# Selective attention followed by a hard-swish MLP: queries of four head pairs in another order, and three loads and one small step moved

## The chip, the cores and the metric

The kernel runs on one core of one Trainium2 chip. The metric is the device time of one execution in microseconds. A core has five engines that work side by side, each through its own instructions in order: PE (matrix multiplication, with PEld for the loading of its weights), DVE (vector operations), ACT (activation functions), POOL (general operations, and the issuing of some transfers) and SP (which issues transfers only). An engine that needs another's result waits for a semaphore. Matrix products land in PSUM, a small memory from which only DVE and ACT copy results to the main on-chip memory, SBUF.

## The reference

The inputs q, k and v have 8 batches, 8 heads, 576 tokens and 64 numbers a token; s has one number per batch, head and token. What is computed, cut to what matters:

```python
scores = q @ k^T / 8
cum = cumsum(max(s, 0))                        # per head, along the tokens
bias = -(cum[query] - cum[key])
scores = where(key > query, -1e9, scores + minimum(bias, 0))
attn = softmax(scores)
x = (attn @ v), heads side by side             # [4608, 512]
h = x @ w_in                                   # [4608, 2048]
out = (h * clip(h + 3, 0, 6) / 6) @ w_out      # [4608, 512]
```

## The kernel before, in words

**Tiling.** The 64 heads are worked on as 32 pairs, p = 0 to 31; a batch has four pairs (PPB = 4). All is in half precision. For a head the scores stand transposed, keys on the partitions and queries along the row: `scores(p, hh, g)` makes them in three parts, g = 0 for the four diagonal blocks of 128 keys by 128 queries, g = 1 and 2 for the blocks beside the diagonal; `corner(p)` makes the last 64 by 64 block of both heads. ACT takes the exponential of each part (L355, L393) into the tile P. `av(p, hh, part)` multiplies P with the values (and a column of ones, which gives the sums), `norm` divides (L434, L435, on DVE), and `transpose_x(p)` turns the result so that it can be the MLP's input xT (five PE transposes, L449, and a DVE copy, L454). In the MLP, `m1` makes one block of 128 features by 512 tokens (L478), ACT and DVE apply the gate (L493, L494), and `m2` multiplies with w_out (L505).

**The mask and the bias.** For p < 8 (NPROD) the causal mask is added by a matmul: `ident2`, twice the identity, times `shut`, a tile of 640 columns that holds -65504 where the key comes after the query (L318 for the four diagonal blocks, L374 for the corner). The bias comes from four extra rows of q and k, on partitions 64 to 67 of the tiles qk: for the queries the cumulative sum and ones, for the keys minus one and the sum in three parts. These rows lie ready for 32 heads in `rows_of` (slot 0 for queries, slot 1 for keys) and `load_aug(p)` fetches them with two transfers, one per head (L151). Pair 0 does without them: its bias comes from matmuls with `picked`, a copy of the query rows with all but one head's rows at zero. `pick(1)` makes the second head's (L712).

**From q and k to the tiles qk.** `load_qk` brings the tokens of a pair in with two transfers (L116). For p < 11 each of 96 partitions holds six tokens in a row per head. `transpose_in` turns them with six PE transposes per operand, two tokens at a time (L242), so that in PSUM the even tokens of each two lie on partitions 0 to 63 and the odd ones on 64 to 127. `transpose_out` then brings them in order with two copies, one for each half (L259): a copy reads a PSUM row in steps and writes every second element of the row of qk. For queries both copies are on DVE. For keys the first is on ACT and the second on DVE; both write to the same stretch of qk, and the second waits for the first. Pair 0 uses `head_out`, which does the same for one head (L273).

**The order of the work** is written out by hand in the loop over p. For p < 4 a pass holds attention alone: scores, `get(0)` (the query copies of pair p + 1), the corner, the last two steps of pair p - 1 (`av`, `norm`), `get(1)` (the key copies of p + 1), the second head's scores, and `transpose_x(p - 1)`. From p = 4 on the steps of the MLP are put between them by `group()`, after a list `plan`. PE, ACT and DVE work through what this order gives them.

**Transfers.** Two queues matter. POOL issues q and k, w_in and w_out and most of the bias rows, and between these it converts V to half precision (`cast_v`, L195 and L196). SP issues V (`load_v`, three transfers per pair, into two buffers in turn, so that V of p + 2 waits for the conversion of p), the bias rows of pairs 2 and 3, and later the outputs. What waits at the head of such a queue holds up all that stands behind it.

Of the kernel before, what the change touches and what calls it, by code (L numbers as in the profile page):

```python
# [18 lines left out]
def kernel(  # L19
# [10 lines left out]
    nc = tc.nc  # L30
# [61 lines left out]
    shut = keep("shut", [128, 640], F16)  # L92
# [3 lines left out]
    rows_of = keep("rows_of", [128, 2, 640], F16, 2)  # L96
# [12 lines left out]
    def load_qk(p, i):  # L109
        b, h0 = p // PPB, 2 * (p % PPB)  # L110
        src = (q, k)[i][b, h0 : h0 + 2]
        if not flat(p):
            if not i:
                tok = work.tile([128, 24 * D], F16, tag="tok", bufs=4, name="tok")
                toks[p] = tok[0:96].rearrange("p (i h e d) -> p i h e d", i=2, h=2, e=6)
            nc.gpsimd.dma_start(  # L116
                out=toks[p][:, i].rearrange("p h e d -> p h (e d)"),
                in_=src.rearrange("h (p e) d -> p h (e d)", e=6),
            )
        else:  # L120
            if p < NSW:
                if not i:
                    tok = work.tile([128, 24 * D], F16, tag="tok", bufs=4, name="tok")
                    toks[p] = tok[:, 0 : 18 * D]
                to, eng = toks[p], nc.gpsimd
            else:
                to, eng = raws[p % NRAW], nc.sync
            eng.dma_start(
                out=to.rearrange("p (i t d) -> p i t d", i=2, t=9)[:, i],
                in_=src.rearrange("h s d -> (h s) d").rearrange(  # L130
                    "(t p) d -> p t d", p=128
                ),
            )
# [14 lines left out]
    def load_aug(p, eng):  # L148
        for hh in range(2):
            g = 2 * p + hh  # L150
            eng.dma_start(  # L151
                out=qks[p % NQK][64:68, hh, :, 64 * hh : 64 * hh + SEQ],
                in_=rows_of[g // 32].rearrange("(r g) i t -> g r i t", g=32)[
                    g % 32, :, :, 0:SEQ
                ],
            )
# [72 lines left out]
    def transpose_in(p, i):  # L229
        tok = toks[p]  # L230
        pt = t_bank(i == 1 and p != NPROD, "pt")
        if flat(p):
            for c in range(5):
                c0 = 512 * i + 128 * c
                nc.tensor.transpose(
                    pt[:, 128 * c : 128 * (c + 1)], tok[:, c0 : c0 + 128], ident
                )
            return pt
        for hh in range(2):
# [8 lines left out]

    def transpose_out(
# [6 lines left out]
        copies = (nc.scalar.copy if i else copies[0], copies[1])  # L256
        for par in pars:
            to = qk[0:64, 0, i, par : par + SEQ]
# [11 lines left out]
    def head_out(p, i, hh, pt, copies):  # L270
        to = qks[p % NQK][0:64, hh, i, 64 * hh : 64 * hh + SEQ]
        for par in range(2):
# [28 lines left out]
    def by_rows(p, hh, out, keys, queries, stop=False):  # L301
        mm(
            out,
            lhsT=rows_of[0][:, 1, keys],
            rhs=picked[:, 2 * p + hh, queries],
            start=False,
            stop=stop,
        )

    def scores(p, hh, g):  # L310
# [4 lines left out]
        if g == 0:  # L315
            rows = slice(0, 68 if by_product else 128)
            if by_product:
                mm(S, lhsT=ident2, rhs=shut[:, 0:512], start=True, stop=False)  # L318
# [13 lines left out]
        else:  # L332
# [10 lines left out]
            if p < NROW:  # L343
                for j in ((0, 3) if g == 1 else (1, 2)):
# [4 lines left out]
                        lhsT=rows_of[0][:, 1, 128 * j : 128 * (j + 1)],  # L349
# [19 lines left out]
    def corner(p):  # L369
# [3 lines left out]
        if by_product:  # L373
            mm(  # L374
                S.rearrange("p h c -> p (h c)"),
                lhsT=ident2,
                rhs=shut[:, 512:640],
# [66 lines left out]
    def transpose_x(p):  # L444
# [3 lines left out]
        for t in range(5):  # L448
# [3 lines left out]
                ident,  # L452
# [155 lines left out]
    fill(nc.gpsimd, shut, 0.0)  # L608
    for c in (slice(0, 512), slice(512, 640)):
        w = 128 if c.start == 0 else 64  # L610
        part = shut[:, c].rearrange("p (t c) -> p t c", c=w)
# [3 lines left out]
            pattern=[[0, (c.stop - c.start) // w], [1, w]],  # L615
# [4 lines left out]
        )  # L620

# [24 lines left out]
    fill(nc.gpsimd, rows_of[0][:, 0, :], 1.0)  # L646
    fill(nc.gpsimd, rows_of[0][:, 1, SEQ:640], 0.0)
# [21 lines left out]
    fill(nc.vector, qks[0][64:68, 0, :, :], 0.0)  # L669

# [15 lines left out]
    def cum3(n, copy, cols):  # L686
        copy(out=rows_of[n][:, 1, cols], in_=C["c"][:, cols])

    def cum4(n, eng, cols):
# [3 lines left out]
            in1=rows_of[n][64:128, 1, cols],  # L693
# [3 lines left out]
    def cum5(n, copy, cols):  # L697
        copy(out=rows_of[n][64:128, 1, cols], in_=C["r"][64:128, cols])

    def cum6(n, eng, cols):  # L700
        lo = rows_of[n][96:128, 1, cols]
# [9 lines left out]
    def pick(g):  # L711
        nc.vector.tensor_scalar(  # L712
            out=picked[:, g, :],
            in0=rows_of[0][:, 0, 0:SEQ],
# [22 lines left out]
    fill(nc.gpsimd, rows_of[0][0:32, 1, 0:SEQ], -1.0)  # L737
# [9 lines left out]
    nc.gpsimd.tensor_copy(out=rows_of[0][0:32, 0, 0:SEQ], in_=C["c"][0:32])  # L747
# [4 lines left out]
    head_out(0, 1, 0, pts[1], (V.tensor_copy, V.tensor_copy))  # L752
    head_out(0, 0, 1, pts[0], (A, V.tensor_copy))
    head_out(0, 1, 1, pts[1], (V.tensor_copy, V.tensor_copy))
    warm(NWARM[2])
    for g in range(1, 2 * NROW):
        pick(g)
# [7 lines left out]
    load_aug(3, nc.sync)  # L765
    cast_v(1)
    for i in range(2):
        load_qk(4, i)

# [3 lines left out]
    for p in range(NP):  # L773
# [9 lines left out]
        if p == 1:  # L783
            load_aug(4, nc.gpsimd)
        elif p == 2:
# [4 lines left out]
        elif p == 3:  # L790
            cast_v(3)
            load_w_in(1)
            qk_ahead()
            load_aug(6, nc.gpsimd)
            cast_v(4)
        elif p:
# [42 lines left out]
        if p and p + 2 < NP:  # L839
            load_v(p + 2, nc.sync)  # L840
        if p == 2:
            nc.sync.dma_start(out=stair_sb, in_=stair_dram.ap())
        if p == 10:
            load_s(1, (nc.sync,) * 4)
            fill(nc.gpsimd, rows_of[1][:, 0, :], 1.0)
# [96 lines left out]
        elif p == 12:  # L942
            nc.scalar.copy(out=rows_of[1][0:32, 0, 0:SEQ], in_=C["c"][0:32])
            cum3(1, nc.scalar.copy, whole)
            fill(nc.gpsimd, rows_of[1][0:32, 1, 0:SEQ], -1.0)
# [44 lines left out]
```

The softmax here doesn't subtract the row's maximum and nothing guards it: scores larger than these inputs give would overflow.

## Time and profile before

| what | value |
|---|---|
| time, median of 3 runs | 356.13 us |
| lowest and highest of the 3 | 356.01 and 356.15 us |
| the profiled run | 356.22 us |
| its span in the trace | 354.5 us |
| clock that PE was granted | 1.00 of full speed |
| passes p = 0 to 3, attention alone | until about 27 us |
| last transfer of w_out that the MLP needs | landed at 61.9 us |

The span is what the trace covers; a run takes some 1.7 us more. A page of the profile gives the busy time of each engine, and then rows of groups of instructions: source line, engine, operation, tile written <- tiles read, the shapes (partitions x elements), the count, and after the bar the busy us in all, the mean ns of one, and the engine's idle us just before them with what ended it. In a timeline a row begins with the start and the length in us, and an idle time before it stands in brackets, with the instruction that ended it.

### The profile page before, as it was taken

To read this page: it belongs to the slowest core of one execution; us is meant where nothing else is said; L and a number is where in the kernel's file an instruction comes from. 1 tells how busy PE (TensorE), PEld (TensorE's weight loads), DVE (VectorE), ACT (ScalarE), POOL (GpSimd) and SP (SyncE) were. 2 spreads that over 40 slices of the span, in tenths; PEclk is the share of its full clock that TensorE was granted. 3 is DMA by queue.
4 is the path that set the end of the run, shared out by engine and by line. 5 is a ranking of instruction groups with operands and counts; after the bars stand their busy time and mean duration, and the time that the engine had idled before them with its cause. 6 is when DMAs were issued, how large, how long until landed. Compare 5 with 4: busy or idle time off the path is not lost.

```text
span 354.5 us, 7771 instructions
## 1 busy us (share of the span) xinstructions
PE 345.6 (97%) x2926; PEld 191.5 (54%) x2926; DVE 231.5 (65%) x472; ACT 225.4 (64%) x397; POOL 169.6 (48%) x295
## 2 busy tenths in 40 slices
PE   7889999999999999999999999999999999999995
PEld 3676666655555555555555555555555444444442
DVE  7898897677878677666666665757654553544531
ACT  6897896787787666667766666666664344433310
POOL 8987799666779556555555555555310000000000
PEclk9999999999999999999999999999999999999999
DMA  9999999999999999998788969997120100101111
GB/s 164 156 219 209 186 184 175 104 187 183 146 126 140 190 219 187 160 214 178 174 176 189 179 162 187 175 176 164 39 75 12 59 31 31 59 2 59 59 58 63
DMA packets 144438, 48.35 MB, mean 136 GB/s; under 512 B 130696, under 2 KB 139432, under 8 KB 144400
## 3 DMA queue, kind: packets, MB, share of 16 engines
q1 hardware_dynamic: 117088, 37.52, 53.4%
q0 software_dynamic: 27072, 10.05, 25.4%
q8 instruction: 23, 0.38, 0.5%
q10 hardware_dynamic: 240, 0.28, 0.2%
q14 instruction: 15, 0.12, 0.1%
HBM read 37.36 MB, written 9.44 MB: 132 GB/s over the span
## 4 chain that ended last, share of the span: by engine, by line
PE 90%; DVE 4%; ACT 3%; issue 1%; DMA 1%; ACTq 0%
PE po L505 34%; PE ph L478 34%; PE O L412 8%; PE S L336 7%; PE S L321 4%; DVE qk L259 1%; PE pt L242 1%; ACT P L355 1%; PE ptx L449 1%; DMA s_all<-in_s_dram 1%; DVE x L435 1%; PE S L318 1%; ACT tr L493 1%; DVE qk L219 1%; PE Sc L385 0%
## 5 line engine op out<-in xcount | busy, mean ns | idle before, releaser
L494 DVE SCALAR_TENSOR_TENSOR gT<-tr,ph 128x512 f16<-128x512 f32 x144 | 98.9, 687 | 97.4 <-ACT tr L493 96.3
L478 PE MATMUL ph<-xT,w_in_sb 128*128 128x512 f16 x576 | 148.1, 379 | 0.0
L505 PE MATMUL po<-w_out_sb,gT 128*128 128x512 f16 x576 | 145.8, 379 | 0.0
L493 ACT ACTIVATE tr<-ph,bias 128x512 f32<-128x512 f32 x144 | 99.1, 688 | 73.0 <-PE ph L478 70.6
L355 ACT ACTIVATE P<-S 128x512 f16<-128x512 f32 x192 | 111.4, 596 | 37.4 <-PE S L321 22.2
L478 PEld LDWEIGHTS <-w_in_sb 128*128 128x128 f16 x576 | 51.6, 97 | 44.2
L505 PEld LDWEIGHTS <-gT 128*128 128x128 f16 x576 | 50.2, 97 | 46.4 <-issue 0.2
L359 POOL TENSOR_SCALAR_AFFINE_SELECT P<-P 128x512 f16<-128x512 f16 x48 | 31.2, 650 | 45.2 <-ACT P L355 45.1
L336 PE MATMUL S<-qk 68*128 68x448 f16 (+3 forms) x256 | 49.0, 272 | 0.3 <-ACT P L355 0.2
L412 PE MATMUL O<-va,P 128*128 128x65 f16 x896 | 47.9, 193 | 0.3 <-ACT P L355 0.3
L412 PEld LDWEIGHTS <-P 128*128 128x128 f16 x896 | 39.3, 97 | 14.0 <-ACT P L355 0.5
L219 DVE COPY qk<-jt 64x768 f16<-64x768 f16 x84 | 36.6, 437 | 1.2
L336 PEld LDWEIGHTS <-qk 68*128 68x128 f16 x256 | 23.7, 98 | 24.2 <-issue 0.7
L151 POOL DMA_DIRECT2D qk<-rows_of x58 | 34.1, 591 | 2.8 <-PE S L336 1.6
L435 DVE TENSOR_TENSOR x<-O,rl 128x320 f16<-128x320 f32 x64 | 31.5, 492 | 2.2
L521 DVE TENSOR_SCALAR ob<-po 128x512 f32<-128x512 f32 (+1 forms) x36 | 24.4, 676 | 8.3 <-PE po L505 7.6
L259 DVE COPY qk<-pt 64x576 f16<-64x576 f16 x30 | 24.0, 805 | 6.4 <-ACT qk L259 5.3
L359 POOL TENSOR_SCALAR_AFFINE_SELECT PC<-PC 128x128 f16<-128x128 f16 x24 | 7.1, 294 | 41.0 <-ACT PC L393 40.9
L321 PEld LDWEIGHTS <-qk 128*128 128x128 f16 (+1 forms) x256 | 18.9, 98 | 12.7 <-DVE qk L259 0.8
L321 PE MATMUL S<-qk 128*128 128x128 f16 (+1 forms) x256 | 24.8, 219 | 0.0
L195 POOL CAST va<-vraw 128x512 f16<-128x512 f32 x32 | 21.2, 664 | 3.4 <-DMA vraw<-in_v_dram 3.3
L191 POOL CAST tok<-raw 128x576 f16<-128x576 f32 x28 | 18.1, 681 | 0.0
(71 smaller groups left out, 197.4 us busy)
## 6 DMA issues: line engine op xcount, KB each, us to landing
out_dram<-ob SPq DMA_DIRECT2D x35, 256.0 KB, 2.2
vraw<-in_v_dram SPq DMA_DIRECT2D x64, 128.0 KB, 3.8
raw<-in_q_dram SPq DMA_DIRECT2D x14, 288.0 KB, 3.7
raw<-in_k_dram SPq DMA_DIRECT2D x14, 288.0 KB
tok<-in_q_dram POOLq DMA_DIRECT2D x18, 144.0 KB, 4.9
tok<-in_k_dram POOLq DMA_DIRECT2D x18, 144.0 KB, 6.0
w_in_sb<-in_moe_w_in_dram POOLq DMA_DIRECT2D x4, 512.0 KB, 8.7
w_out_sb<-in_moe_w_out_dram POOLq DMA_DIRECT2D x8, 256.0 KB, 7.4
```

The source lines that it names most:

```text
L151: eng.dma_start(out=qks[p % NQK][64:68, hh, :, 64 * hh : 64 * hh + SEQ], in_=rows_of[g // 32].rearrange("(r g) i t -> g r i t", g=32)[g % ...
L219: copies[par](out=qk[0:64, :, i, 128 * par : 128 * par + 256 * n].rearrange("p h (s two c) -> p h s two c", two=2, c=128)[:, :, :, 0, :], ...
L321: mm(S[:, c], lhsT=kT[rows, c], rhs=qT[rows, c], start=(j == 0 and not by_product), stop=(j == 3 and p >= NROW),)
L336: mm(S[:, c : c + w], lhsT=kT[0:68, 128 * j : 128 * (j + 1)], rhs=qT[0:68, 128 * (j + 1) : SEQ], start=(c == 0), stop=(c != 0 and p >= NROW),)
L355: nc.scalar.activation(out=pt[:, c], in_=S, func=AF.Exp, scale=0.125)
L359: nc.gpsimd.affine_select(out=part, in_=part, pattern=[[0, part.shape[1]], [1, w]], compare_op=ALU.is_ge, fill=0.0, base=0, channel_multip ...
L412: mm(o[:, i, :], lhsT=lhsT, rhs=va[:, hh, j, 0:65], **kw)
L435: nc.vector.tensor_tensor(out=X[p][:, :, hh, :], in0=o[:, :, 0:64], in1=rl.to_broadcast([128, 5, 64]), op=ALU.mult,)
L478: mm(ph, lhsT=w_in_sb[:, kc, ft * 128 : (ft + 1) * 128], rhs=xT[:, kc, n * 512 : (n + 1) * 512], start=(kc == 0), stop=(kc == NKC - 1),)
L493: nc.scalar.activation(out=tr, in_=ph, func=AF.Relu, bias=bias3[:, 0:1])
L494: nc.vector.scalar_tensor_tensor(out=gTs[n][:, ft, :], in0=tr, scalar=6.0, in1=ph, op0=ALU.min, op1=ALU.mult)
L505: mm(po, lhsT=gTs[n][:, ft, t4 * 128 : (t4 + 1) * 128], rhs=w_out_sb[:, ft, :], start=(ft == 0), stop=(ft == NFT - 1),)
```

## The change

It has four parts.

1. **Queries of pairs p = 3 to 6 in another order.** `mixed(p, i)` is true for i = 0 (queries) and these pairs. `load_qk` now puts four tokens in a row on each partition, three times, both heads as one run of 1152 tokens. The six PE transposes write runs of 16 columns in steps of 32, and the two copies out of PSUM read one contiguous row and write runs of 16. Within each group of 64 queries, token 4v + w then stands at place 16w + v. The order of the keys stays. The mask in this order is a second tile, `shutm`; the query rows of the bias in this order are a third slot of `rows_of` (slot 0 is now the new order, 1 the old, 2 the keys), written by a POOL copy. In `transpose_x` the identity is replaced by a permutation matrix `perm`, which puts the queries back. The mask tiles shrink to 128 columns and are read four times (or twice, 64 columns) in one matmul.
2. **Keys of pairs p = 2, 4 and 6.** The first copy, which was one ACT copy of both heads, becomes an ACT copy of head 1 and a DVE copy of head 0.
3. **The second picking** moves ahead of the copies of pair 0's second head.
4. **Queues.** On SP the bias rows of pair 3 no longer stand ahead of V of pair 3, but behind it, and are followed by the rows of pair 4, which POOL issued before. On POOL the second part of w_in moves behind the tokens and rows of pair 6.

```diff
-    shut = keep("shut", [128, 640], F16)
+    shut, shutm = keep("shut", [128, 128], F16, 2)
+    perm = keep("perm", [128, 128], F16)
-    rows_of = keep("rows_of", [128, 2, 640], F16, 2)
+    rows_of = keep("rows_of", [128, 3, 640], F16, 2)
...
+            if mixed(p, i):
+                nc.gpsimd.dma_start(
+                    out=toks[p][:, i]
+                    .rearrange("p h e d -> p (h e d)")
+                    .rearrange("p (t x) -> p t x", t=3),
+                    in_=src.rearrange("h s d -> (h s) d").rearrange(
+                        "(t p e) d -> p t (e d)", p=96, e=4
+                    ),
+                )
+                return
...
-                    g % 32, :, :, 0:SEQ
+                    g % 32, :, slice(0, 3, 2) if mixed(p, 0) else slice(1, 3), 0:SEQ
...
+        if mixed(p, i):
+            for t in range(3):
+                for c in range(2):
+                    nc.tensor.transpose(
+                        pt[:, 0:SEQ].rearrange("p (g c v) -> p c g v", c=2, v=16)[
+                            :, c, 6 * t : 6 * t + 6
+                        ],
...
+    def mixed(p, i):
+        return i == 0 and PPB - 1 <= p < NPROD - 1
...
-        copies = (nc.scalar.copy if i else copies[0], copies[1])
+        if i and (p % 2 or p >= NPROD):
+            copies = (nc.scalar.copy, copies[1])
+        elif i:
+            head_out(p, i, 1, pt, (nc.scalar.copy,), (0,))
+            head_out(p, i, 0, pt, (nc.vector.tensor_copy,), (0,))
+            pars = (1,)
         for par in pars:
+            if mixed(p, i):
+                to = qk[0:64, 0, i, 16 * par : 16 * par + SEQ]
+                copies[par](
+                    out=bass.AP(
+                        to.tensor,
+                        to.offset,
+                        [list(to.ap[0]), [2 * SPAD + 64, 2], [32, 18], [1, 16]],
+                    ),
+                    in_=pt[64 * par : 64 * par + 64, 0:SEQ].rearrange(
+                        "p (h g v) -> p h g v", h=2, v=16
+                    ),
+                )
+                continue
...
-                mm(S, lhsT=ident2, rhs=shut[:, 0:512], start=True, stop=False)
+                mm(
+                    S.rearrange("p (t c) -> p t c", c=128),
+                    lhsT=ident2,
+                    rhs=(shutm if mixed(p, 0) else shut)[:, None, :].to_broadcast(
+                        [128, 4, 128]
+                    ),
...
-                ident,
+                perm if mixed(p, 0) else ident,
...
+    make_shut(shut, shut, [[1, 128]])
+    make_shut(shutm, mix(shutm), [[64, 2], [1, 4], [4, 16]])
+    nc.gpsimd.tensor_copy(out=unmix(perm), in_=mix(ident))
...
     fill(nc.vector, qks[0][64:68, 0, :, :], 0.0)
+    fill(nc.vector, rows_of[0][:, 0, :], 1.0)
...
     head_out(0, 1, 0, pts[1], (V.tensor_copy, V.tensor_copy))
+    for g in range(1, 2 * NROW):
+        pick(g, V)
     head_out(0, 0, 1, pts[0], (A, V.tensor_copy))
     head_out(0, 1, 1, pts[1], (V.tensor_copy, V.tensor_copy))
     warm(NWARM[2])
-    for g in range(1, 2 * NROW):
-        pick(g)
...
     load_v(2, nc.sync)
-    load_aug(3, nc.sync)
     cast_v(1)
     for i in range(2):
         load_qk(4, i)
+    nc.gpsimd.tensor_copy(
+        out=mix(rows_of[0][0:32, 0, 0:SEQ]), in_=unmix(C["c"][0:32])
+    )
...
-        if p == 1:
-            load_aug(4, nc.gpsimd)
-        elif p == 2:
+        if p == 2:
...
             cast_v(3)
-            load_w_in(1)
             qk_ahead()
             load_aug(6, nc.gpsimd)
+            load_w_in(1)
             cast_v(4)
...
             load_v(p + 2, nc.sync)
+        if p == 1:
+            load_aug(3, nc.sync)
+            load_aug(4, nc.sync)
```

## The prediction

> Pairs are counted by the index p of the code, from 0; the regrouped queries are those of p = 3 to 6. An arrow gives times before and after the change; the times after are all worked out here.
>
> **What bounds the kernel now.** First the page's busy shares, then busy time by stretch, cut where PE starts a pair's scores.
>
> ```profile
> PE 345.6 (97%) x2926; PEld 191.5 (54%) x2926; DVE 231.5 (65%) x472; ACT 225.4 (64%) x397; POOL 169.6 (48%) x295
> ...
> 14.26:18.42 4.16, 3.77 (x74) 3.04 (x71) 3.62 (x7) 4.01 (x9) 3.63 (x7) 1.00 1.25 217
> 18.42:22.68 4.26, 3.81 (x75) 3.02 (x71) 4.08 (x9) 3.84 (x9) 4.26 (x8) 1.00 1.24 214
> 22.68:26.94 4.26, 3.80 (x74) 3.01 (x70) 4.08 (x9) 3.84 (x9) 2.69 (x6) 1.00 1.25 219
> ...
> 120.00:340.00 220.00, 220.00 (x1654) 116.28 (x1653) 132.54 (x261) 130.23 (x221) 74.28 (x138) 1.00 0.60 122
> ```
>
> The columns are the stretch, its length, then busy us of PE, PEld, DVE, ACT and POOL. From 42 us on PE is the bound; in the attention-only stage it isn't, DVE is fullest. Busy PE hides waits, so I summed start-to-start times of consecutive matmuls less columns/2.4 + 2.5 ns: 338.4 us of work and 10.0 us of slack, of which 3.25 lie before 10 us, 1.57 in 10 to 20, 1.64 in 20 to 30, 1.04 in 30 to 40, and 2.5 in all the rest. A change that takes no matmul away can only get at these.
>
> Second, the timeline of DVE over one such pair, p = 2:
>
> ```profile
> 18.63 0.46 DVE L454 COPY xT<-ptx 128x576 f16<-128x576 f16 x1
> 19.01 0.18 DVE L434 RECIPROCAL rl<-O 128x5 f32<-128x5 f32 x1
> 19.23 0.49 DVE L435 TENSOR_TENSOR x<-O,rl 128x320 f16<-128x320 f32 x1
> 19.64 1.63 DVE L259 COPY qk<-pt 64x576 f16<-64x576 f16 x2
> 21.30 0.20 DVE L434 RECIPROCAL rl<-O 128x5 f32<-128x5 f32 x1
> 21.53 0.49 DVE L435 TENSOR_TENSOR x<-O,rl 128x320 f16<-128x320 f32 x1
> 22.05 0.81 DVE L259 COPY qk<-pt 64x576 f16<-64x576 f16 x1
> 22.89 0.46 DVE L454 COPY xT<-ptx 128x576 f16<-128x576 f16 x1
> ```
>
> No wait stands in it: the items fill 18.63 to 22.89, exactly the 4.26 us period. ACT waits 0.42 us a pair for the scores. Third, what PE waits for:
>
> ```profile
> 11.93 0.19 PE L302 MATMUL Sc<-w_out_sb,rows_of 128*128 128x64 f16 x1 [0.65 <-DVE w_out_sb L712]
> ...
> 22.07 0.28 PEld L449 LDWEIGHTS <-x 128*128 128x128 f16 x5 [0.72 <-DVE x L435]
> ...
> 26.33 0.28 PEld L449 LDWEIGHTS <-x 128*128 128x128 f16 x5 [0.73 <-DVE x L435]
> ```
>
> The first is p = 0's corner waiting for the second picking (L712). The others are the transposes of x, waiting for a normalisation that stands on DVE behind the two query copies. In matmul starts these gaps are 0.82, 0.61 and 0.62 us, with one of 0.55 at 17.19.
>
> Last, the rows with durations by shape:
>
> ```profile
> L259 DVE COPY qk<-pt 64x576 f16<-64x576 f16 x30 | 24.0, 805 | 6.4 <-ACT qk L259 5.3 <-PE pt L242 0.6
> L454 DVE COPY xT<-ptx 128x576 f16<-128x576 f16 x9 | 4.1, 454 | 0.6 <-PE ptx L449 0.5
> L273 DVE COPY qk<-pt 64x288 f16<-64x288 f16 x5 | 2.4, 480 | 0.6 <-ACT qk L273 0.5
> ```
>
> L259 and L454 copy 576 half-precision elements out of PSUM. The one whose rows run on takes 454 ns, the one that steps through both sides 805.
>
> **What the Trainium skill says.** "VectorE: DVE Perf Modes", section "Why PSUM operands drop a tier": a PSUM source allows at most the packed mode of two results a cycle. "Vector Engine (DVE) Microarchitecture Reference", section 5.1, gives the condition: every tensor of 2 bytes with innermost step one. L454 against L259 agrees, 351 ns apart; that runs of 16 are enough on the written side no row here shows. "TensorE: Matmul & The Clock Gate", section "Wait — 56ns, not 53.3ns?": warm matmuls start every N/2.4 + 2.5 ns; from 270 to 340 us the slack by that formula is under 0.05 us in all, so it holds. Its Part 4: a transpose is in.T @ identity; a permutation in the identity's place keeps the shape, so I take the 219 ns of L449 and no change in spacing. The six query transposes (L242) stay six of 96 columns; that they now write runs of 16 I cost at nothing, since PE waits for DVE right behind them.
>
> **The change, part by part.**
>
> *Queries, p = 3 to 6.* Two DVE copies a pair now read a contiguous PSUM row and write runs of 16. Their spacing is 0.815 us (1.63/2); in packed mode I take L454's 0.454 and 0.01 between: 0.70 us less per pair. Bounds: 0.93 less, were one copy 0.35 (at the 0.96 GHz of the skill's DVE page, two a cycle, the elements alone are 0.30); nothing less, if runs of 16 miss the mode. They run in the loop pass before their own pair: passes 2, 3, 4, 5.
>
> *Keys, p = 2, 4, 6.* The first half of the key copy, 0.80 us on ACT, becomes one head on ACT (0.47, L273) and one on DVE (0.48 to 0.50): ACT wins 0.33, DVE loses 0.50. The second half on DVE, which waits for both, may start 0.33 sooner where ACT was the last.
>
> *Second picking.* L712 (0.57 us) moves ahead of head 1's copies. DVE idles 0.46 us there (waiting for ACT's copy), ahead of the copies at 9.77, so it starts at 9.30, ends at 9.87 and pushes them by 0.07.
>
> *Masks, perm, rows.* PE's mask matmuls keep 512 and 128 columns: nothing. On POOL at the start 1.33 us of filling and selecting become about 1.15 (two fills of 0.15, two selects of 0.29, a copy like them). Were the three-level select twice as slow, the next loads would slip 0.1 us, against 0.9 of margin for tok of p = 1 (landed 9.29, read 10.24). The new fill of rows_of on DVE (0.33, as L177's 0.30 for 288 words) lands in the 0.35 us that DVE waits before the scan at 4.72: nothing, at most 0.05. The regrouped bias rows cost POOL one cast, 0.68 (L747) to perhaps 1.5; it takes the place of two 0.59 issues of p = 4's rows.
>
> *Sync and POOL queues.* V of p = 3 goes out when its buffer is freed, 14.27 → about 13.35. Behind it stand rows of 3, which now wait for POOL's cast (about 15.6), rows of 4, then V of 4 (17.37 → 18.0) and the stair. Rows of 3 then land near 20 (3.3 us, the median of these transfers) and are read at 22.5. V of 4 landed at 25.9, so now near 26.5; read at 30.4. The second w_in load moves behind tok and rows of 6, in a queue that lands its transfers in order: 29.89 → about 31.5, read at 35.7 less the gain. The regrouped query loads have 288 pieces for 192; tok of 5 and 6 arrive 4 to 5 us early. All of it is hidden.
>
> *The path.* p = 0: PE goes on when head 1's copies are done, 11.35, so the next transposes start 11.96 → 11.45: **-0.51**. p = 1: DVE starts the queries of 2 at 15.38 → 14.88, but its chain gets 0.50 of keys, and the copy that the scores of 2 await ends at 18.61 as before: **+0.51**, and ACT waits longer. p = 2: normalisation 22.02 → 21.27, so PE transposes when its own work is done, at 21.47. The keys' second half then waits for ACT's whole first half, done at 21.57 as before, and ends 22.86 → 22.41: **-0.45**. p = 3: 0.70 less and 0.50 more on DVE, while ACT follows with 0.33 less: **-0.20**. p = 4: the gaps at 31.25 (0.50) and 33.31 (0.29) come from ACT's order behind PE's own matmuls; they shift along. p = 5: the gate product stood behind 1.61 us of query copies, and PE lost 0.15 at 39.15 for its bank: **-0.15**. Sum: **-0.80 us**, on the profiled span 354.5 → 353.7. That run took 356.22, 1.7 above its span; the median is 356.13, so I forecast **355.3**.
>
> **Rivals.**
> - *More.* PE's gaps of p = 4 close too (up to 0.79), or p = 1 hides its extra key copy. For it: DVE gets free there. Against: ACT's row. -1.5, so 354.6.
> - *No net gain.* ACT, at 3.84 of 4.26, becomes the bound in passes 2 and 3 and what p = 2 wins is lost to the key copies: 356.1.
> - *Slower: the packed mode is missed in L259's place.* Each regrouped copy stays at 0.80. Then p = 0 and 1 cancel, p = 2 wins 0.03 and p = 3 pays 0.47: +0.4, so 356.6. It decides from where a copy takes over about 0.69 us (0.50 = 2 x 0.25 saved). For it: eighteen runs by two heads are no single row. Against: 16 is even and the source runs on.
> - *The second w_in load comes late.* PE would stand at about 35.0 for each us after that; the load would have to slip 3.5 us more. +0.5 or more.
>
> **How the numbers follow.** Forecast 0.50, more 0.20, no net gain 0.10, packed mode missed 0.16, late load 0.04. What can be told from no change is 0.2%, 0.71 us, so the forecast lies just beyond it: two thirds of its chance (0.33) count as faster, 0.17 as no change. Faster 0.53, same 0.27, slower 0.20. Alone, the forecast's range is 354.9 to 355.8; the 8-in-10 range takes in most of the larger gain and the missed mode: 354.5 to 356.6.
>
> **What would show it.** Regrouped copies of 64x576 near 0.45 us; no wait on L712 in p = 0; scores of p = 2 where they started before, near 18.7, those of 3 near 22.0 to 22.5, those of 4 near 26.3; PE's waits for x gone in passes 2 and 3 but not in 1; everything after 42 us shifted as one. A copy near 0.8, or scores of 4 at 27 or later, makes it wrong; so does a PE wait for a transfer.

## The result, and the profile after

| | before | after |
|---|---|---|
| time, median | 356.12 us (356.01 to 356.15) | 354.75 us (354.51 to 354.79) |
| the profiled run | 356.22 us | 354.79 us |
| its span | 354.5 us | 353.1 us |
| start of the last matmul | 349.75 us | 348.75 us |
| from there to the end of the span | 4.76 us | 4.32 us |

The ratio is 0.9961, with a 95% interval of 0.9943 to 0.9978 (ratios, here and below, are of mean times; the times are medians). The kernel became 1.37 us (0.4%) faster, where 0.8 us was forecast: 354.75 lies inside the 8-in-10 range, and just below the forecast's own range (354.9 to 355.8).

The page's busy shares, and busy time by stretch, again cut where PE starts the scores of p = 1, 2, 3 and 4 (columns as before: the stretch, its length, busy us of PE, PEld, DVE, ACT, POOL):

```profile
PE 345.1 (98%) x2926; PEld 191.0 (54%) x2926; DVE 230.2 (65%) x476; ACT 224.7 (64%) x397; POOL 169.7 (48%) x296
...
13.58:17.74 4.16, 3.77 (x74) 3.07 (x71) 3.64 (x8) 4.01 (x9) 3.98 (x6) 1.00 1.24 197
17.74:21.73 3.99, 3.77 (x74) 3.08 (x71) 3.54 (x9) 2.99 (x8) 3.94 (x7) 1.00 1.24 201
21.73:25.55 3.82, 3.78 (x75) 3.09 (x71) 3.66 (x10) 3.82 (x9) 2.63 (x5) 1.00 1.24 215
```

The stretch of p = 2 is 3.99 us long where it was 4.26, that of p = 3 3.82 where it was 4.26; the stretch of p = 1 is as long as before, 4.16. A cut stands at the mask's matmul, ahead of the first product of keys and queries, so a wait for keys falls at the head of the next stretch. Since busy PE hides waits, the prediction's count is the better measure (start to start, less columns/2.4 + 2.5 ns). By it the gaps ahead of the transposes of x in passes 1, 2 and 3, which were 0.55, 0.61 and 0.62 us, are 0.55, 0 and 0. In their place gaps of 0.38, 0.20 and 0.36 us stand at the first scores of p = 2, 3 and 4, each of them waiting for a key copy.

DVE, which filled its stretch at p = 2 (4.08 of 4.26), now has 3.54 of 3.99 and waits there for ACT's key copy. In pass 3 it is full again, with the key copy that the split gives it (L332):

```profile
21.29 0.81 DVE L310 COPY qk<-pt 64x576 f16<-64x576 f16 x1 [0.31 <-ACT qk L310]
22.13 0.46 DVE L523 COPY xT<-ptx 128x576 f16<-128x576 f16 x1
...
23.13 0.91 DVE L298 COPY qk<-pt 64x576 f16<-64x576 f16 x2
...
24.77 0.47 DVE L332 COPY qk<-pt 64x288 f16<-64x288 f16 x1
25.26 0.81 DVE L310 COPY qk<-pt 64x576 f16<-64x576 f16 x1
26.10 0.46 DVE L523 COPY xT<-ptx 128x576 f16<-128x576 f16 x1
```

From 22.13 to 26.10 there is no wait in it. These 3.97 us are also the time from the first scores of p = 3 to those of p = 4.

The groups of copies, with their durations (rows by shape; after the bar the busy us, the mean ns of one, the idle time before):

```profile
L310 DVE COPY qk<-pt 64x576 f16<-64x576 f16 x22 | 17.6, 805 | 6.2 <-ACT qk L310 5.9 <-PE pt L266 0.2
L523 DVE COPY xT<-ptx 128x576 f16<-128x576 f16 x9 | 4.1, 454 | 0.6 <-PE ptx L518 0.5
L332 DVE COPY qk<-pt 64x288 f16<-64x288 f16 x8 | 3.8, 478 | 0.5 <-ACT qk L332 0.3
L298 DVE COPY qk<-pt 64x576 f16<-64x576 f16 x8 | 3.6, 450 | 0.5 <-PE pt L253 0.4
```

L310 is the old L259, L523 the old L454, L332 the old L273. L298 is the regrouped query copy: 450 ns, as short as the copy whose rows run on, though it writes runs of only 16 elements. The condition that the Trainium skill gives for the packed mode in "Vector Engine (DVE) Microarchitecture Reference", section 5.1 (two-byte types, innermost step one, and more than one element in the innermost row), is met by runs of 16, and this row agrees with it.

What PE waits for between 9 and 40 us (us in total, times, longest):

```profile
PE S L388 <- DVE qk L332: 0.5, 1, 0.5
PE S L388 <- DVE qk L310: 0.4, 2, 0.2
PE ptx L518 <- DVE x L504: 0.4, 1, 0.4
PE O L481 <- ACT P L422: 0.3, 1, 0.3
PE S L403 <- ACT P L422: 0.3, 1, 0.3
```

The wait on the second picking is gone, and two of the three waits for the normalisation (L504, the old L435) too. The first line is the wait of p = 0's first scores at 9.29 us; by the count above this gap is anything from under 0.1 to 0.73 us in the traces below, whatever was changed. New are the waits for L310 and, in the last line, one of L403 on ACT.

**Where the time came from.** Both traces hold the same 2926 matmuls in the same order, so each can be set against its counterpart. The table gives the shift of some of them. The first scores differ by -0.16 to +0.10 us among all the traced executions below, also where nothing ahead of them is changed, so "from there" takes that first shift off; "step" is the difference from the row above. Negative is sooner. "Scores" are the first product of keys and queries of a pair.

| matmul | before, us | shift | from there | step | forecast |
|---|---|---|---|---|---|
| first scores, p = 0 | 9.36 | -0.07 | 0 | | |
| corner, p = 0 | 11.96 | -0.69 | -0.62 | -0.62 (p = 0) | -0.51 |
| scores of p = 2 | 18.66 | -0.32 | -0.25 | +0.37 (p = 1) | +0.51 |
| scores of p = 3 | 22.92 | -0.76 | -0.69 | -0.44 (p = 2) | -0.45 |
| scores of p = 4 | 27.19 | -1.06 | -0.99 | -0.30 (p = 3) | -0.20 |
| beside the diagonal, in p = 4 | 33.63 | -0.85 | -0.78 | +0.21 (p = 4) | 0 |
| first product of the MLP, p = 5 | 39.34 | -1.00 | -0.92 | -0.15 (p = 5) | -0.15 |
| last matmul | 349.75 | -1.00 | -0.92 | 0.00 | 0 |

The two traced spans differ by 1.43 us. PE's path gives 0.92 of it, for the 0.80 forecast, and the shift of the first scores 0.07. The other 0.44 us come after the start of the last matmul, where nothing was forecast. There SP closes the program (the closing, from here on) with eight waits on the semaphores that its and ACT's transfers raise, always in the same order; each of them also waits for a second semaphore, which had been raised over 2 us before. Their times, from the records of SP's queue of instructions, with the semaphore that the last output transfer raises in brackets:

```
wait on semaphore   before     after
100                 352.45    350.79
102                [352.83]   351.06
104                 352.90    351.49
105                 352.99   [351.90]
106                 353.06    351.97
107                 353.44    352.03
108                 353.52    352.09
109                 353.58    352.15
last landing        352.81    351.89
end of span         354.50    353.07
```

The last transfer lands 3.07 us after the start of the last matmul before, 3.14 after. But from the landing to the wait on 109 it is 0.77 us before, in seven waits, and 0.26 after, in five. SP's and ACT's transfers take these eight semaphores in turn (a pair of records around the end: 109, 100, 102 before; 102, 104, 105 after), and the change put two more transfers on SP.

Two waits fewer, of some 0.065 us, make only 0.13 us of that difference. Another 0.33 is a single wait: 107 comes 0.39 us after 106 before, and 0.06 after. It is the 336th record of SP's queue, and in the nine traces of fourteen (those below included) in which SP has nothing else to wait for at its 336th record, SP is idle for 0.36 to 0.38 us just there. In the kernel after this record is the wait on 100, ahead of the last landing, where it costs nothing: five more records stand ahead of the closing. Why this place is slow no run shows.

### The profile page after: what moved, and what is told of

Its sections match the earlier page's. It is cut to its first block, busy times and chain, and to the rows that moved or that the text cites. A ratio compares the mean times of both kernels' runs of the same rounds, so it can differ in the third digit from the quotient of the medians.

```text
span 353.1 us, 7778 instructions
## 1 busy us (share of the span) xinstructions
PE 345.1 (98%) x2926; PEld 191.0 (54%) x2926; DVE 230.2 (65%) x476; ACT 224.7 (64%) x397; POOL 169.7 (48%) x296
## 4 chain that ended last, share of the span: by engine, by line
PE 90%; DVE 4%; ACT 3%; issue 1%; DMA 1%; ACTq 0%
PE po L574 35%; PE ph L547 34%; PE O L481 7%; PE S L403 7%; PE S L388 4%; DVE qk L310 1%; PE pt L266 1%; ACT P L422 1%; DMA s_all<-in_s_dram 1%; DVE x L504 1%; PE ptx L518 1%; PE Sc L454 1%; ACT tr L562 1%; PE S L377 1%; DVE qk L332 1%
## 5 line engine op out<-in xcount | busy, mean ns | idle before, releaser
L422 ACT ACTIVATE P<-S 128x512 f16<-128x512 f32 x192 | 111.3, 595 | 37.5 <-PE S L388 22.3
L426 POOL TENSOR_SCALAR_AFFINE_SELECT P<-P 128x512 f16<-128x512 f16 x48 | 31.3, 651 | 44.4 <-ACT P L422 44.4
L403 PE MATMUL S<-qk 68*128 68x448 f16 (+3 forms) x256 | 49.0, 272 | 0.5 <-ACT P L422 0.5
L403 PEld LDWEIGHTS <-qk 68*128 68x128 f16 x256 | 23.7, 98 | 24.5 <-issue 0.9
L162 POOL DMA_DIRECT2D qk<-rows_of x56 | 32.8, 588 | 1.1 <-PE S L403 0.3
L504 DVE TENSOR_TENSOR x<-O,rl 128x320 f16<-128x320 f32 x64 | 31.5, 492 | 2.2
L426 POOL TENSOR_SCALAR_AFFINE_SELECT PC<-PC 128x128 f16<-128x128 f16 x24 | 7.0, 293 | 39.9 <-ACT PC L462 39.8
L310 DVE COPY qk<-pt 64x576 f16<-64x576 f16 x22 | 17.6, 805 | 6.2 <-ACT qk L310 5.9
```

The costliest lines, as they stand in the source:

```text
L162: eng.dma_start(out=qks[p % NQK][64:68, hh, :, 64 * hh : 64 * hh + SEQ], in_=rows_of[g // 32].rearrange("(r g) i t -> g r i t", g=32)[g % ...
L403: mm(S[:, c : c + w], lhsT=kT[0:68, 128 * j : 128 * (j + 1)], rhs=qT[0:68, 128 * (j + 1) : SEQ], start=(c == 0), stop=(c != 0 and p >= NROW),)
L422: nc.scalar.activation(out=pt[:, c], in_=S, func=AF.Exp, scale=0.125)
L426: nc.gpsimd.affine_select(out=part, in_=part, pattern=[[0, part.shape[1]], [1, w]], compare_op=ALU.is_ge, fill=0.0, base=0, channel_multip ...
L504: nc.vector.tensor_tensor(out=X[p][:, :, hh, :], in0=o[:, :, 0:64], in1=rl.to_broadcast([128, 5, 64]), op=ALU.mult,)
```

## The experiments

My theory had three parts: (A) in the attention-only stage DVE decides, and the regrouped copies, the picking and the split of keys add up there as in the table; (B) the step of +0.21 at p = 4 is a wait of ACT on DVE that the change brought in; (C) the shorter closing comes from the number of transfers alone. The rivals: the new order isn't what helps; the split pays through ACT; the closing differs by chance. Each kernel was run beside the kernel before, whose medians were 356.11, 356.01 and 356.13 us in the three groups below.

### First group: the parts alone, and the new order off

**The picking alone**, on the kernel before:

```diff
+    for g in range(1, 2 * NROW):
+        pick(g)
     head_out(0, 0, 1, pts[0], (A, V.tensor_copy))
     head_out(0, 1, 1, pts[1], (V.tensor_copy, V.tensor_copy))
     warm(NWARM[2])
-    for g in range(1, 2 * NROW):
-        pick(g)
```

> The kernel before with the second picking alone moved ahead of the copies of head 1. Theory (the step at p = 0 is the wait on the picking, and it is lost again at p = 1 only because of the key copy that pair 2 puts on DVE): PE's corner of p = 0 starts about 0.5 to 0.7 us sooner, and without the split of keys everything behind it shifts as one, so the last matmul ends 0.5 to 0.7 sooner, with the closing behind it (last matmul to end of span) at 4.75 as before: about 355.5. Rival (the gain is swallowed in p = 1 by ACT or by PE's own waits, whatever the keys do): last matmul within 0.1 of before, 356.1.

355.48 us, ratio 0.9983 (0.9976 to 0.9989). The shift from the first scores is -0.61 at the corner of p = 0, -0.61 at the scores of p = 2, -0.62 at those of p = 4 and -0.65 at the last matmul: all of it is kept. The closing is as before. The theory holds; what p = 1 takes back in the changed kernel is not owed to PE's or ACT's own waits.

DVE's timeline shows why the step is larger than forecast. Before:

```profile
8.33 0.97 DVE L273 COPY qk<-pt 64x288 f16<-64x288 f16 x2
9.77 1.51 DVE L273 COPY qk<-pt 64x288 f16<-64x288 f16 x3 [0.46 <-ACT qk L273]
11.31 0.57 DVE L712 TENSOR_SCALAR w_out_sb<-rows_of,sel 128x576 f16<-128x576 f16 x1
11.91 0.79 DVE L259 COPY qk<-pt 64x576 f16<-64x576 f16 x1
```

With the picking alone moved:

```profile
8.27 0.97 DVE L273 COPY qk<-pt 64x288 f16<-64x288 f16 x2
9.27 0.37 DVE L712 TENSOR_SCALAR w_out_sb<-rows_of,sel 128x576 f16<-128x576 f16 x1
9.71 1.51 DVE L273 COPY qk<-pt 64x288 f16<-64x288 f16 x3
11.25 0.81 DVE L259 COPY qk<-pt 64x576 f16<-64x576 f16 x1
```

The picking, 572 ns where it stood, takes 370 ns in the new place, which lies whole in the 0.46 us that DVE waited for ACT. The copies behind it aren't pushed back by 0.07, as I had forecast, and come when they came before.

**The queues alone**, on the kernel before:

```diff
     load_v(2, nc.sync)
-    load_aug(3, nc.sync)
...
-        if p == 1:
-            load_aug(4, nc.gpsimd)
-        elif p == 2:
+        if p == 2:
...
-            load_w_in(1)
             qk_ahead()
             load_aug(6, nc.gpsimd)
+            load_w_in(1)
...
+        if p == 1:
+            load_aug(3, nc.sync)
+            load_aug(4, nc.sync)
```

> The kernel before with the four moves on the queues alone: bias rows of pair 3 behind V of 3 on SP, rows of pair 4 on SP instead of POOL, second part of w_in behind tokens and rows of pair 6. Theory (all these loads are hidden, but two more transfers on SP shift which semaphore the last output transfer raises, and so how many waits of the closing come after it): matmul starts within 0.05 us of before everywhere, closing 4.75 to about 4.3: 355.7. Rival one (the shorter closing has nothing to do with this part): 356.1, closing 4.75. Rival two (the loads were part of the gain of PE): matmul starts of p = 3 or 4 sooner by 0.2 or more.

355.63 us, ratio 0.9985 (0.9978 to 0.9991). The first scores stand at -0.16, and from there no matmul in the table moves by more than 0.03: the moved loads give PE nothing and cost it nothing. From the end of the last matmul to the end of the span it is 3.87 us, before 4.38.

**The same number of transfers, without any move**: on the kernel before, the load of one 64 KB tile (the stair tile, `stair_sb`) in three transfers.

```diff
-            nc.sync.dma_start(out=stair_sb, in_=stair_dram.ap())
+            for a, z in ((0, 64), (64, 96), (96, 128)):
+                nc.sync.dma_start(out=stair_sb[a:z], in_=stair_dram.ap()[a:z])
```

> The kernel before, with only the load of the stair tile (same bytes) cut into three transfers on SP, that is two more, as many as the change adds. Theory (only the count of transfers decides on which semaphore the last output transfer falls): matmul starts as before within 0.05 us, last output transfer raises semaphore 105 instead of 102, closing 4.75 to about 4.3, 355.7. Rival (the shorter closing comes from the change's other parts, or differs by chance from run to run): closing 4.75, 356.1.

355.63 us, ratio 0.9987 (0.9981 to 0.9994). From the first scores to 62 us the matmuls move by -0.06 at most, by -0.09 at the last. The last output transfer raises 105, and the span ends 3.94 us after the last matmul's end. A kernel with not one instruction of the changed part in it thus gains the same 0.48 us by median as the moves of the queues. Part C holds: transfers added to SP's queue are enough, by the semaphore that the last one raises and by where in SP's queue the closing begins.

**The new order off**, with all else as in the kernel after:

```diff
     def mixed(p, i):
-        return i == 0 and PPB - 1 <= p < NPROD - 1
+        return False
```

> The kernel after with the new order of queries switched off for all pairs; keys of 2, 4, 6, second picking and queues as after. Theory (DVE bounds the stage, and only the two copies of 0.45 instead of 0.80 us pay for the key copies that it gets): p = 0 and 1 as after (-0.3 at the end of p = 1), p = 2 wins almost nothing and p = 3 loses about 0.5, so the matmuls from p = 4 on stand 0.1 to 0.4 later than before, and with the closing at 4.35: about 355.9 to 356.1. Rival (the new order isn't what helps; the picking and the split of keys are): matmuls of p = 4 on 0.8 to 1.0 sooner, 354.75.

355.74 us, ratio 0.9990 (0.9983 to 0.9996). The steps: p = 0 -0.63, p = 1 +0.37, p = 2 -0.01, p = 3 +0.34, and nothing behind; the last matmul stands at +0.03 from the first scores, where the kernel after has -0.92. What is left of the gain is the closing (3.87 us). This is also what a missed packed mode would have done to the path, by the rival that I had priced at +0.4: it is +0.05, since p = 0 and 1 leave -0.26 and p = 3 costs 0.34 and not 0.47. PE's waits for the normalisation are all three there again:

```profile
PE ptx L518 <- DVE x L504: 1.3, 3, 0.4
PE S L388 <- DVE qk L310: 0.4, 2, 0.2
PE O L481 <- ACT P L422: 0.3, 1, 0.3
```

So the new order carries 0.95 us beside the split of keys, and the picking and the split without it cancel.

### Second group: the two steps that cost, and the closing

**Pair 2's keys as before**, on the kernel after:

```diff
-        if i and (p % 2 or p >= NPROD):
+        if i and (p % 2 or p == 2 or p >= NPROD):
             copies = (nc.scalar.copy, copies[1])
```

> The kernel after, but the keys of pair 2 copied as before (first half on ACT for both heads, nothing more on DVE). Theory (p = 1 gives 0.37 of the gain back because DVE is full there and gets one more copy): the scores of p = 2 start 0.65 to 0.70 sooner than before instead of 0.32, later steps stay, closing as after; last matmul about 0.35 sooner than after: 354.4. Rival (the split pays through ACT, which gets 0.33 free in p = 1 and needs it in p = 2): the gain at p = 1 is lost again by the scores of p = 3 or 4; 354.7 or more.

354.42 us, ratio 0.9959 (0.9947 to 0.9972), 1.59 us under the kernel before. The step at p = 1 is +0.02 in place of +0.37; p = 2, 3, 4 and 5 give -0.44, -0.30, +0.21 and -0.15, as in after. The timeline of DVE in p = 1 shows what the split puts in the way. After:

```profile
16.60 0.49 DVE L504 TENSOR_TENSOR x<-O,rl 128x320 f16<-128x320 f32 x1
17.00 0.46 DVE L332 COPY qk<-pt 64x288 f16<-64x288 f16 x1
17.48 0.80 DVE L310 COPY qk<-pt 64x576 f16<-64x576 f16 x1
18.32 0.46 DVE L523 COPY xT<-ptx 128x576 f16<-128x576 f16 x1
```

With pair 2's keys as before:

```profile
16.52 0.49 DVE L504 TENSOR_TENSOR x<-O,rl 128x320 f16<-128x320 f32 x1
17.05 0.81 DVE L310 COPY qk<-pt 64x576 f16<-64x576 f16 x1
17.89 0.46 DVE L523 COPY xT<-ptx 128x576 f16<-128x576 f16 x1
```

The copy that the scores of p = 2 await starts at 17.05 instead of 17.48. ACT won 0.33 us by the split, and then stood idle for 1.00 us before the first exponential of p = 2, because those scores came late (before: 0.42 us):

```profile
15.83 0.48 ACT L332 COPY qk<-pt 64x288 f16<-64x288 f16 x1
16.26 1.57 ACT L422 ACTIVATE P<-S 128x512 f16<-128x512 f32 x3
18.84 1.57 ACT L422 ACTIVATE P<-S 128x512 f16<-128x512 f32 x3 [1.00 <-PE S L388]
```

**All keys as before** (no pair is split), on the kernel after:

```diff
-        if i and (p % 2 or p >= NPROD):
+        if i:
             copies = (nc.scalar.copy, copies[1])
```

> The kernel after with the keys of all three pairs (2, 4, 6) copied as before. Theory (where the queries are in the new order DVE has 0.70 us a pair to spare and the split frees ACT of 0.33, so it pays in p = 3; where they aren't, it costs): the scores of p = 2 start 0.65 to 0.70 sooner than before, those of p = 3 about 1.1, and at p = 3 the step of -0.30 of after shrinks to -0.1 to 0, so that the result lies between after and the run with only pair 2's keys as before: 354.5 to 354.7. Rival (the split never pays): the step at p = 3 stays, and it is as fast as the run with pair 2's keys alone as before or faster, 354.4 or less.

354.43 us, ratio 0.9957 (0.9944 to 0.9969). My expectation missed: the result isn't between the two, and the step at p = 3 grew where it was to shrink. The scores of p = 4 come 0.16 us sooner than with the split (step -0.46 in place of -0.30; the gap at them is 0.16 us in place of 0.36), and what follows loses that again, with a new gap of 0.25 us at 26.36, where PE waits for an exponential of ACT: at 39.34 the shift from the first scores is -1.28, and -1.31 with only pair 2's keys as before. The split of pairs 4 and 6 moves nothing in sum; the split of pair 2 costs 0.35. Since the picking alone stands at -0.61 at that matmul and the queues move none, the new order without any split is worth 0.67 us there: part of the 0.95 above pays for the split. Part A thus holds for the picking and the regrouped copies; the split is a cost.

**Pair 5's queries in the old order**, on the kernel after:

```diff
     def mixed(p, i):
-        return i == 0 and PPB - 1 <= p < NPROD - 1
+        return i == 0 and p in (3, 4, 6)
```

> The kernel after, without the new order for pair 5 (its queries, mask, bias rows and transposes of x as before). Theory (the step of +0.21 at p = 4, forecast as 0, is there because ACT's copy of pair 5's keys waits for DVE's regrouped copy of pair 5's queries, a wait that the kernel before hasn't): with that wait gone the scores of p = 5 start about 1.06 sooner than before instead of 0.85, and about 0.2 is kept: 354.55. Rival (DVE's two shorter copies in p = 4 are needed, or the 0.21 is ACT's own order behind PE): the shift at p = 4 stays at 0.85 or less; 354.75 or more.

354.49 us, ratio 0.9955 (0.9942 to 0.9969), 1.52 us under the kernel before. The step at p = 4 is -0.01, and from the first scores the last matmul stands at -1.17 (after: -0.92). ACT's timeline shows the wait that is gone. After, the key copy of pair 5 (L310) starts 0.35 us behind the start of the corner's exponential:

```profile
31.12 0.29 ACT L462 ACTIVATE PC<-Sc 128x128 f16<-128x128 f32 x1
31.47 0.80 ACT L310 COPY qk<-pt 64x576 f16<-64x576 f16 x1
32.14 0.58 ACT L422 ACTIVATE P<-S 128x512 f16<-128x512 f32 x1
```

With pair 5 in the old order it starts 0.16 us behind, as it did before the change (32.18 and 32.34):

```profile
31.12 0.29 ACT L462 ACTIVATE PC<-Sc 128x128 f16<-128x128 f32 x1
31.28 0.80 ACT L310 COPY qk<-pt 64x576 f16<-64x576 f16 x1
31.93 0.59 ACT L422 ACTIVATE P<-S 128x512 f16<-128x512 f32 x1
```

In the kernel after, this ACT instruction waits for PE and for DVE's regrouped copy (L298, 30.93 to 31.38); in the kernel before and in this one, for PE alone. Keys and queries of a pair are different parts of one tile, so the data don't ask for that wait. Only argued, not shown, is that it comes from the way in which the regrouped copy describes what it writes: the key copy of pair 3, which has the new order too, waits for PE alone at 20.44 us. What is shown is that it comes and goes with the new order of this pair. With it goes what PE loses in p = 4 to ACT's exponential (L403, 0.33 us idle at 32.78): the gap there is 0.28 us in place of 0.49, and was 0.29 before. Part B holds.

**The closing, four transfers further**: on the kernel after, the 64 KB load in five transfers.

```diff
-            nc.sync.dma_start(out=stair_sb, in_=stair_dram.ap())
+            for a, z in ((0, 32), (32, 64), (64, 96), (96, 112), (112, 128)):
+                nc.sync.dma_start(out=stair_sb[a:z], in_=stair_dram.ap()[a:z])
```

> The kernel after with the load of the stair tile (same bytes) cut into five transfers on SP, four more, so that the last output transfer raises the semaphore that the closing waits for last (109 instead of 105). Theory (each wait that stands behind the last transfer's own costs about 0.065 us once it has landed): four waits fewer, -0.26: 354.5, with matmul starts as after. Rival (the closing is bound by the landing of the last transfer and by what follows the waits, whichever semaphore it raises): 354.75.

354.50 us (354.36 to 355.57), ratio 0.9966 (0.9953 to 0.9979). The matmuls stand as in after (-0.99 at the last from the first scores). The last transfer raises 109, lands at 351.72, and the wait on 109 follows at 351.74 as the last of the eight; from the end of the last matmul to the end of the span it is 3.58 us, and 3.94 and 3.87 in the two traces of after. By the trace the four waits are worth 0.3 us; the times spread too widely to show it by themselves.

### Third group: do the repairs add up?

The first kernel is the one after, unchanged, beside the others.

> The kernel after, unchanged, beside the next three on one chip. Expected -1.37 us to before as in the first runs, so about 354.7.

354.62 us (354.60 to 355.41), ratio 0.9962 (0.9950 to 0.9974).

**Both costs undone**: pair 2's keys as before and pair 5's queries in the old order, that is, the two diffs above together.

> The kernel after with the two parts undone that were seen to cost: pair 2's keys copied as before, and pair 5's queries in the old order. Theory (the two costs, 0.37 at p = 1 and 0.21 at p = 4, stand in different passes and add up): matmuls behind p = 5 about 0.55 to 0.6 sooner than in after, 354.15. Rival (they share a resource, so that the second one gives nothing once the first is gone): 354.4.

354.35 us, ratio 0.9962 (0.9949 to 0.9974). On PE's path they do add up: from the first scores, the matmuls at 62 us stand at -1.52, and at -0.96 in the trace of after beside it; 0.15 us of that is lost again by the last matmul (-1.37). But the times don't follow: of 22 runs 13 lie between 354.07 and 354.48, the other nine anywhere up to 358.28. The kernel before stayed within 356.01 to 356.38 in 27 runs.

**No split, and pair 5's queries in the old order:**

> As the run before it, but with the keys of pairs 4 and 6 copied as before too (no pair is split). Theory (the split pays nothing in pairs 4 and 6, as the earlier pair of runs, 354.42 and 354.43, showed): the same within 0.1, 354.15. Rival (with pair 5's wait gone ACT's 0.33 in pairs 4 and 6 counts): 0.2 or more slower, 354.35 or more.

354.52 us (354.22 to 355.92), ratio 0.9959 (0.9946 to 0.9973). -1.48 at 62 us, as the run before within 0.04, and then a loss of 0.88 at one place.

**Both costs undone, and the 64 KB load in five transfers:**

> The run with the two parts undone, and the stair tile loaded with five transfers instead of one. Theory (the shorter closing adds to what PE gains): closing shorter by 0.29, as in the earlier trace (3.87 to 3.58 from the end of the last matmul), so 353.9. Rival (the four more transfers delay V or bias rows once PE is ahead, or the closing of that run was chance): the same as without them, 354.15, or slower.

354.30 us (353.83 to 355.37), ratio 0.9951 (0.9939 to 0.9963). The closing is 3.58 us, as expected, and the matmuls at 62 us stand at -1.50. The traced run, one of 355.37 us, then loses 1.52 us at one place. PE's waits there, in its timeline:

```profile
62.66 0.32 PE L481 MATMUL O<-va,P 128*128 128x65 f16 x5
63.39 0.30 PE L481 MATMUL O<-va,P 128*128 128x65 f16 x4 [0.41 <-POOL P L426]
64.43 0.20 PE L481 MATMUL O<-va,PC 128*128 128x65 f16 x1 [0.74 <-POOL PC L426]
```

PE waits for POOL, which from p = 8 on applies the causal mask to P (L426). POOL's timeline in the same trace:

```profile
56.97 2.45 POOL L695 COPY qk<-stair_sb 64x1280 f16<-64x1280 f16 x2
59.37 1.20 POOL L162 DMA_DIRECT2D qk<-rows_of  x2
60.56 1.07 POOL L139 DMA_DIRECT2D tok<-in_q_dram  x1
61.61 1.04 POOL L139 DMA_DIRECT2D tok<-in_k_dram  x1
62.70 0.63 POOL L426 TENSOR_SCALAR_AFFINE_SELECT P<-P 128x512 f16<-128x512 f16 x1
```

The mask stands behind 5.7 us of copies and DMA issues without a gap. In the trace of the kernel with both costs undone the same row of copies starts at 54.06, 2.9 us sooner, and the mask is done at 60.42. POOL's place in its program thus differs by some 3 us between these two traces (by 0.7 us between the two of the kernel after), with the landing of the transfers it waits for: here the conversion of V of pair 5, at 32.50, had waited 2.45 us, in that other trace not at all. For this one wait the rival of the expectation offers a cause: the four added transfers stand ahead of V of pair 5 in SP's queue. In the two kernels that have them on top of the change this V is issued at 25.7 and 25.8 us, and its conversion waits 3.42 and 2.45 us; in the other eight traces of the kernel after and its variants it is issued at 21.4 to 22.3 us, and the conversion waits at most 0.78. But the first of the two has its masks in time, so this isn't the whole of it. In the kernel after the masks of P and PC were done at 61.25 and 62.29 and read at 63.23 and 63.51, a margin of 1.2 us at the second, and of 0.45 in its other trace; each 0.5 us that PE wins takes as much off it. Of the traces of this group and the second one, the three with the mask of P done after 62.6 us are the three that lose time at 64 us: 0.40 us in the kernel with all keys as before, 0.88 and 1.52 in the last two.

So no version here is shown to be faster than the kernel after: the intervals of the last one and of after beside it overlap. The repairs are real on PE's path and are taken back, in three of the traces, by a wait that neither trace of the kernel after has. That the slow executions without a trace have the same cause is likely, but not shown; one of the five runs of the kernel after in this group, at 355.41 us, is among them. What makes the landings differ between executions, and whether a V transfer sent sooner would cure it, wasn't tried.

## Why the prediction was right, and where it wasn't

**Right in sign and in the mechanism.** Regrouped copies of 450 ns (454 assumed) take 0.70 us a pair from DVE; that is worth 0.44 at p = 2 (0.45 forecast) and carries p = 3; p = 5 gives 0.15 as forecast. The signs that I had asked for are there: no wait on the picking; PE's waits for x gone in passes 2 and 3 and not in 1; scores of p = 3 at 22.16 (22.0 to 22.5 forecast); one shift for everything behind 42 us; no new wait of PE for a transfer. Switching the new order off takes 0.95 us of it back. That the path comes so close to its sum is in part luck: p = 0, 1 and 3 give 0.35 us more than forecast, and p = 4 takes 0.21 away.

**p = 0 and p = 1: size off.** "-0.51" was -0.62 and "+0.51" was +0.37, so that the two leave -0.25 where I had 0. The term at p = 0 was built on the picking's 0.57 us from its row; in the new place it takes 0.37 and needs nothing but the gap. At p = 1 the added key copy takes 0.48 us on DVE, but it starts 0.40 us after the start of the normalisation ahead of it, where the old copy there started 0.53 after: 0.13 less than the sum of the durations. Scores of p = 2 thus came at 18.34, not near 18.7.

**p = 3: size off.** -0.30 for -0.20. DVE decides there as forecast; from start to start its query copies take 0.73 us less (0.70 forecast), and the added key copy 0.44 more (0.50 forecast).

**p = 4: a step that failed.** "They shift along" was wrong: +0.21, from a wait of ACT for DVE that the diff doesn't show and that I hadn't looked for. Undoing pair 5 alone takes it away.

**The queues: the other step that failed.** "All of it is hidden" is true of the loads themselves (the queues alone move no matmul by more than 0.03 us). But I counted the two additional transfers on SP only for the time that they take there, and not for what they do to the closing, through the semaphore that the last transfer raises and the place of the waits in SP's queue: 0.44 us of the 1.43 between the traces come from that, and the 64 KB load in three transfers brings the same without the change.

**The rivals.** "More" named 354.6, close to the result, but for reasons that the runs don't bear out: PE's gaps of p = 4 did not close, one grew, and p = 1 didn't hide its key copy. "No net gain" through ACT didn't come: what p = 2 wins is kept, and ACT idles 1.00 us at p = 2. It is close, though: ACT is busy in all 3.82 us of the stretch of p = 3. The missed packed mode is answered by the row of 450 ns. The late load of w_in didn't show: PE doesn't wait for it in the trace of the kernel after.

## What to carry to other kernels

Cost a moved instruction by what may run beside it in its new place, not by its old row alone, and give work to an engine only in the stretch where it has been freed: the same split of keys cost 0.35 us in the pair ahead of the regrouped ones and nothing where the copies were short. When an access pattern changes form, look for new waits between engines in the changed kernel, also between parts of one tile that don't overlap. And before crediting a fraction of a microsecond to a change, compare the end of the last matmul with the end of the span: here two transfers more moved the closing by 0.44 us, half of what the change gave on PE's path.

## What was not expected of the hardware

- The closing costs 1.69 us from the last landing to the end of the span when the last transfer raises the second of the eight semaphores waited for (102), 1.18 at the fourth (105) and 0.92 at the last (109). Most waits that find their transfer done take 0.06 to 0.09 us each; the 336th record of SP's queue took 0.38 to 0.40 in nine traces, although its transfer had landed over 3.5 us earlier: on 107 before and in the kernel with the picking alone, on 100 in seven others. Why is open.
- The picking, one DVE instruction of 128x576 elements out of SBUF, takes 555 to 587 ns at 11.2 to 11.3 us (three traces) and 369 to 371 ns at 9.2 to 9.4 us (eleven traces). At the later time a conversion on POOL (11.16 to 11.47 us) and the issue of two transfers run beside it; at the earlier one POOL starts issuing bias rows. That POOL's work slows it is a guess; no run took that work away.
- The regrouped cast of the bias rows on POOL, 32x576 elements from single to half precision, took 1242 ns (0.68 to 1.5 estimated), nearly twice the 0.68 of the cast in order.
